# A two-layer decode step: layernorm applied after the matmul instead of before it, larger weight transfers, and a later start for part of the last weights

## Chip, cores, metric

One core of a Trainium2 chip. The metric is the device time of one execution in microseconds (us). "Span" is the part of it that the profile covers; it is some 1.7 us shorter. Ratios are the mean time of one kernel's fast runs over the mean of the fast runs of the kernel before in the same rounds on the same chip, so they are not quite the ratio of the medians that are quoted.

## The reference

Four blocks on one token x of width 1024, each with a residual: attention A, MLP B, A, B, both passes with the same weights.

```python
x = x + A(layernorm(x)); x = x + B(layernorm(x))     # pass 1
x = x + A(layernorm(x)); x = x + B(layernorm(x))     # pass 2
# A: q = xhat @ wq (32 heads of 128); softmax over the last 4096 cached keys of
#    4 kv heads; o @ wo
# B: h = xhat @ w1 + b1 (3584 wide); h * tanh(softplus(h)), called mish; @ w2
# layernorm(x) = (x - mean) / sqrt(var + 1e-5)
```

## The kernel before

PE is the matrix engine, DVE the vector engine, ACT or ScalarE the engine for functions; the sync engine (SP) issues transfers. Everything is matrix times vector: PE loads a 128x128 block of weights and multiplies it with one column; such a load with its multiplication is called a pair. wq, K, V and 20 of the 32 row blocks of wo stay in SBUF; the rest of wo, and w1 and w2, are streamed in both passes. The sync engine issues all loads in one order. Pass 1 streams through a ring of eight slots of 512 KB; in pass 2 w1 and w2 go to places that have come free: wq's (after Q), K's (after the scores), V's (after the weighted sum).

```python
# a layernorm: sums by ScalarE and DVE, a ones matmul, ten DVE steps, then Q or W1
T[f"p_lnsum{l}"] = pe.sig(p.matmul(PB_M[:, 0:2], lhsT=ones_f[:, :], rhs=st01, ...))
... # DVE: var, rsqrt by shift and two Newton steps
T[f"v_xhat{l}"] = ve.sig(v.scalar_tensor_tensor(out=xhat(l), in0=xin, scalar=MEAN,
        in1=st(8).to_broadcast([128, DC]), op0=ALU.subtract, op1=ALU.mult))
...
def emit_q(p):
    p.wait_ge(ve.sem, T[f"v_xhat{l}"])
    for j in range(DC):
        ...
        for b in range(H):
            ins = p.matmul(PB_Q[:, j * H + b:j * H + b + 1], lhsT=wq_blk(j, b),
                           rhs=XH[:, j:j + 1], start=True, stop=True)
...
# transfers
P1_K = [add_ring_piece(f"k{q}", k_piece_src(q), 16 * 128, ...) for q in range(8)]   # 512 KB
for j in range(DC):
    for half in range(2):                                  # w1 rows: 4 KiB and 3 KiB
        src, n = w1_src(j, half)
        P1_W1.append(add_ring_piece(f"w1a_{j}_{half}", src, n))
...
    elif jp < n_wq + 8:                                    # w2 of pass 2, into K's place
        dst, waits = kT_sb[:, o:o + 2048], [("T", "p_s1")]   # p_s1: scores of pass 2 done
```

## Time and profile before

| | before |
|---|---|
| median device time | 168.82 us (four runs, 168.65 to 168.88) |
| span of the profiled run | 167.1 us |
| PE / DVE / ACT busy | 53% / 19% / 8% |
| read from HBM | 57.7 MB, 345 GB/s over the span |

The span falls into two parts with different limits. Up to the last W2 piece of pass 1 (105.75 us) PE waits for data; from there on the chain that ends last has no transfer in it. The lines that show it are in the prediction below. In the lines of the chain the columns are start, duration, and what the chain went through; "issue" is an engine that waits for nothing the profile can name.

### The profile page before, as it was taken

To read this page: it belongs to the slowest core of one execution; us is meant where nothing else is said; L and a number is where in the kernel's file an instruction comes from. 1 tells how busy PE (TensorE), PEld (TensorE's weight loads), DVE (VectorE), ACT (ScalarE), POOL (GpSimd) and SP (SyncE) were. 2 spreads that over 40 slices of the span, in tenths; PEclk is the share of its full clock that TensorE was granted. 3 is DMA by queue.
4 is the path that set the end of the run, shared out by engine and by line. 5 is a ranking of instruction groups with operands and counts; after the bars stand their busy time and mean duration, and the time that the engine had idled before them with its cause. 6 is when DMAs were issued, how large, how long until landed. Compare 5 with 4: busy or idle time off the path is not lost.

```text
span 167.1 us, 5451 instructions
## 1 busy us (share of the span) xinstructions
PE 89.4 (53%) x2579; PEld 81.4 (49%) x2579; DVE 31.9 (19%) x108; ACT 13.5 (8%) x23; POOL 1.1 (1%) x11
## 2 busy tenths in 40 slices
PE   2242337956729653355433444464762963749393
PEld 1242337745718652354323333364761863749392
DVE  1400002343164000320022000330116400140402
ACT  3000000565220000000000000000001100000000
POOL 2000000000000000000000000000000000000000
PEclk9999999999655555555555555555555555555555
DMA  3999999999999999999999999999999999960000
GB/s 96 420 433 420 422 375 409 421 429 414 397 388 386 386 383 393 403 391 398 408 388 388 387 391 383 387 388 393 407 405 402 388 386 387 385 240 4 0 8 0
DMA packets 21105, 58.03 MB, mean 347 GB/s; under 512 B 1627, under 2 KB 1627, under 8 KB 19547
## 3 DMA queue, kind: packets, MB, share of 16 engines
q1 hardware_dynamic: 21082, 57.69, 89.6%
q8 instruction: 20, 0.33, 0.8%
q14 instruction: 3, 0.02, 0.0%
HBM read 57.68 MB, written 0.00 MB: 345 GB/s over the span
## 4 chain that ended last, share of the span: by engine, by line
DMA 39%; PE 30%; SPq 10%; DVE 8%; issue 7%; ACT 5%; DVEq 0%
DMA ring<-in_B_w_dram 18%; DMA ring<-in_A_k_cache_dram 13%; DMA wo_sb<-in_A_wo_dram 9%; PE psb L522 6%; SPq L662 5%; PE psb L565 4%; ACT kT_sb L614 4%; PE psb L333 4%; PE psb L599 4%; PE psb L483 3%; SPq L645 2%; PE psb L350 2%; PE psb L445 2%; PE psb L473 2%; SPq L678 2%
## 5 line engine op out<-in xcount | busy, mean ns | idle before, releaser
L333 PE MATMUL psb<-misc_b,wq_sb 128*128 128x1 bf16 x512 | 15.2, 165 | 18.6 <-DMA wq_sb<-in_A_wq_dram 14.1
L333 PEld LDWEIGHTS psb<-misc_b,wq_sb 128*128 128x128 bf16 x512 | 14.4, 104 | 19.4 <-DMA wq_sb<-in_A_wq_dram 12.2
L565 PE MATMUL psb<-act_sb,ring 128*128 128x1 bf16 x224 | 8.0, 166 | 12.1 <-DMA ring<-in_B_w_dram 9.5
L522 PE MATMUL psb<-misc_b,ring 128*128 128x1 bf16 x252 | 8.7, 166 | 10.6 <-DMA ring<-in_B_w_dram 6.3
L483 PE MATMUL psb<-misc_b,wo_sb 128*128 128x1 bf16 x320 | 9.5, 165 | 7.7 <-DMA wo_sb<-in_A_wo_dram 5.1
L522 PEld LDWEIGHTS psb<-misc_b,ring 128*128 128x128 bf16 x252 | 7.7, 105 | 11.6 <-DMA ring<-in_B_w_dram 7.1
L565 PEld LDWEIGHTS psb<-act_sb,ring 128*128 128x128 bf16 x224 | 7.0, 105 | 13.2 <-DMA ring<-in_B_w_dram 10.5
L599 PE MATMUL psb<-misc_b,ring 128*128 128x128 bf16 x128 | 10.9, 251 | 4.4 <-ACT kT_sb L614 3.6
L483 PEld LDWEIGHTS psb<-misc_b,wo_sb 128*128 128x128 bf16 x320 | 9.0, 104 | 8.0 <-DMA wo_sb<-in_A_wo_dram 5.3
L599 PEld LDWEIGHTS psb<-misc_b,ring 128*128 128x128 bf16 x128 | 9.1, 114 | 6.1 <-ACT kT_sb L614 5.1
L614 ACT ACTIVATE kT_sb<-psb 128x1024 bf16<-128x1024 bf16 x8 | 8.2, 1024 | 31.1 <-PE psb L599 31.1
L350 PE MATMUL psb<-misc_b,kT_sb 128*128 128x8 bf16 x256 | 7.3, 168 | 3.6 <-issue 3.1
L350 PEld LDWEIGHTS psb<-misc_b,kT_sb 128*128 128x128 bf16 x256 | 7.1, 104 | 3.9 <-issue 3.3
L445 PEld LDWEIGHTS psb<-et_sb,v_sb 128*128 128x128 bf16 x256 | 7.5, 105 | 1.0 <-issue 0.8
L445 PE MATMUL psb<-et_sb,v_sb 128*128 128x8 bf16 x256 | 7.6, 168 | 0.0
L609 DVE COPY kT_sb<-psb 128x1024 bf16<-128x1024 bf16 x8 | 5.5, 692 | 8.7 <-PE psb L599 8.7
L473 PE MATMUL psb<-misc_b,ring 128*128 128x1 bf16 x192 | 5.7, 165 | 2.7 <-issue 2.0
L473 PEld LDWEIGHTS psb<-misc_b,ring 128*128 128x128 bf16 x192 | 5.4, 104 | 3.0 <-issue 2.1
L359 DVE TENSOR_REDUCE misc_b<-psb 128x32 bf16<-128x256 f32 x2 | 0.8, 425 | 29.7 <-PE psb L333 29.7
L522 PE MATMUL psb<-misc_b,wq_sb 128*128 128x1 bf16 x196 | 5.5, 165 | 0.1
L522 PEld LDWEIGHTS psb<-misc_b,wq_sb 128*128 128x128 bf16 x196 | 5.4, 104 | 0.2 <-issue 0.2
L574 DVE TENSOR_REDUCE psb<-psb 128x8 f32<-128x224 f32 x2 | 0.8, 400 | 23.9 <-PE psb L565 23.9
(75 smaller groups left out, 54.8 us busy)
## 6 DMA issues: line engine op xcount, KB each, us to landing
ring<-in_B_w_dram SPq DMA_DIRECT2D x23, 512.0 KB, 10.1
wq_sb<-in_A_wq_dram SPq DMA_DIRECT2D x8, 1024.0 KB, 12.7
ring<-in_A_wo_dram SPq DMA_DIRECT2D x12, 512.0 KB, 10.6
wo_sb<-in_A_wo_dram SPq DMA_DIRECT2D x5, 1024.0 KB, 14.3
ring<-in_A_k_cache_dram SPq DMA_DIRECT2D x8, 512.0 KB, 21.6
v_sb<-in_A_v_cache_dram SPq DMA_DIRECT2D x4, 1024.0 KB, 18.7
wq_sb<-in_B_w_dram SPq DMA_DIRECT2D x8, 512.0 KB, 9.4
kT_sb<-in_B_w_dram SPq DMA_DIRECT2D x8, 512.0 KB, 10.7
```

Source lines behind the costliest of these rows:

```text
L333: ins = p.matmul(PB_Q[:, j * H + b:j * H + b + 1], lhsT=wq_blk(j, b), rhs=XH[:, j:j + 1], start=True, stop=True)
L350: ins = p.matmul(bank[:, col:col + HPG], lhsT=kT_blk(g, c), rhs=QT[:, g * HPG:(g + 1) * HPG], start=True, stop=True)
L445: ins = p.matmul(PB_O0[:, g * HPG:(g + 1) * HPG], lhsT=v_blk(g, c), rhs=et_sb[:, ecol:ecol + HPG], start=(c == 0), stop=(c == C - 1))
L473: ins = p.matmul(PB_Y[:, col:col + 1], lhsT=pc["dst"][:, o:o + 128], rhs=OT[:, j:j + 1], start=(jj == 0), stop=(jj == 1))
L483: ins = p.matmul(PB_Y[:, col:col + 1], lhsT=wo_res_blk(j, b2), rhs=OT[:, j:j + 1], start=(jj == 0), stop=(jj == 3))
L522: ins = p.matmul(PB_Q[:, j * FC + b:j * FC + b + 1], lhsT=pc["dst"][:, o:o + 128], rhs=XH[:, j:j + 1], start=True, stop=True)
L565: ins = p.matmul(PB_Y[:, j * DC + b2:j * DC + b2 + 1], lhsT=pc["dst"][:, o:o + 128], rhs=ACT_T[:, j:j + 1], start=True, stop=True)
L599: ins = p.transpose(tbk[:, k * 128:(k + 1) * 128], pc["dst"][:, o:o + 128], ident_b)
L609: T[f"v_kev{i}"] = ve.sig(v.tensor_copy(kT_sb[:, dst0:dst0 + 1024], tbk[:, 0:1024]))
L614: T[f"a_kev{i}"] = ae.sig(a.activation(kT_sb[:, dst0:dst0 + 1024], tbk[:, 0:1024], ACTF.Copy))
L645: sp.dma_start(wq_sb[:, j * 4096:(j + 1) * 4096], A_wq[j * 128:(j + 1) * 128, :]).then_inc(sem_wq[j], 16)
L662: sp.dma_start(wo_sb[:, u * 4096:(u + 1) * 4096].rearrange("p (j n) -> p j n", j=4), A_wo[u * 512:(u + 1) * 512, :].rearrange("(j p) n -> ...
```

## The change

The intent is to take the layernorm's serial DVE steps off the way between two matmuls. Since xhat = rstd * x - rstd * mean, Q and W1 can be multiplied with the raw x, and mean and rstd applied to the result; this needs the column sums of wq and w1, which a second moving column of ones delivers in pass 1 and which are kept for pass 2. Along with it come larger transfers (w1 in 896 KB, K in 1 MB, in a ring addressed by column), and one added wait. I call them (a) layernorm, (c) transfers, (d) gate; the small added DVE work is (b).

```diff
-            T[f"v_xhat{l}"] = ve.sig(v.scalar_tensor_tensor(out=xhat(l), ...))
+            T[f"v_xb{l}"] = ve.sig(v.tensor_copy(xb2(l)...[:, 0, :], xin))      # (a) raw x, before the sums
+            ve.sig(v.tensor_reduce(st01[:, 0:1], xin, AX.X, ALU.add))            # was on ScalarE
...
-            p.wait_ge(ve.sem, T[f"v_xhat{l}"])
+            nt = 2 if la == 0 else 1
+            p.wait_ge(ve.sem, T[f"v_xb{l}"])
...
+                t = ve.sig(v.tensor_reduce(QRED, PB_Q..., AX.X, ALU.add))
+            T[f"v_qt{la}"] = ve.sig(v.scalar_tensor_tensor(out=QT, in0=QRED, scalar=ln_rstd(), in1=TMPQ,
+                                                           op0=ALU.mult, op1=ALU.add))   # (b)
...
-    for j in range(DC):
-        for half in range(2):
-            src, n = w1_src(j, half)
-            P1_W1.append(add_ring_piece(f"w1a_{j}_{half}", src, n))
+    P1_W1 = [add_ring_piece(f"w1a_{j}", w1_src(j), FF) for j in range(DC)]       # (c)
+    P1_K = [add_ring_piece(f"k{g}", k_piece_src(g), C * 128, ...) for g in range(G)]
...
-            dst, waits = kT_sb[:, o:o + 2048], [("T", "p_s1")]
+            dst, waits = kT_sb[:, o:o + 2048], [("T", "p_s1"), ("T", "p_wou1_0")]   # (d)
```

`p_wou1_0` is the first of the five resident units of pass 2's output projection.

More of the change, by code (lines that the diff above doesn't have):

```diff
@@ L25 @@
 MISH_CLAMP = 20.0
-NSLOT = 8
 WO_RES = 20
-SLOT = 2048
+RING_COLS = 16384
+NSEM_RING = 12
+STAGE_COLS = 256
 class _Eng:
@@ L53, in _build @@
     v_sb = E(nc.sbuf_tensor("v_sb", [128, G * C * DH], BF16))
-    ring = E(nc.sbuf_tensor("ring", [128, NSLOT * SLOT], BF16))
+    ring = E(nc.sbuf_tensor("ring", [128, RING_COLS], BF16))
     ones_f = E(nc.sbuf_tensor("ones_f", [128, 128], F32))
-    misc_b = E(nc.sbuf_tensor("misc_b", [128, 512], BF16))
-    misc_f = E(nc.sbuf_tensor("misc_f", [128, 320], F32))
+    misc_b = E(nc.sbuf_tensor("misc_b", [128, 576], BF16))
+    misc_f = E(nc.sbuf_tensor("misc_f", [128, 448], F32))
     act_sb = E(nc.sbuf_tensor("act_sb", [128, 2 * FC], BF16))
@@ L62, in _build @@
     ident_b = misc_b[:, 128:256]
-    MB_XH = 256
+    MB_XB2 = 512
     MB_QT = 288
@@ L79, in _build @@
     MF_DD = 286
+    MF_CSQ = 320
+    MF_CS1 = 352
+    MF_TMPQ = 380
+    MF_BB = 412
     def cfc(i):
@@ L86, in xT, with xb2 @@
         return misc_f[:, MF_XS + i * DC:MF_XS + (i + 1) * DC]
-    def xhat(l):
-        return misc_b[:, MB_XH + l * DC:MB_XH + (l + 1) * DC]
+    def xb2(l):
+        return misc_b[:, MB_XB2 + l * 2 * DC:MB_XB2 + (l + 1) * 2 * DC]
     PB = [E(nc.psum_tensor(f"psb{i}", [128, 512], F32)) for i in range(8)]
@@ L102, in _build @@
     XS_RED2 = 496
+    XS_QRED = 96
     pe = _Eng(E(nc.semaphore("sem_pe")))
@@ L112, in _build @@
     sem_wo = [E(nc.semaphore(f"dma_wo{i}")) for i in range(WO_RES // 4)]
-    sem_slot = [E(nc.semaphore(f"dma_slot{i}")) for i in range(NSLOT)]
+    sem_ring = [E(nc.semaphore(f"dma_ring{i}")) for i in range(NSEM_RING)]
     sem_dbg = E(nc.semaphore("dma_dbg")) if dbg is not None else None
@@ L117, in _build @@
     pieces = []
-    ring_count = [0]
+    ring_pieces = []
+    ring_state = dict(off=0)
     def add_ring_piece(name, src, ncols, shape3=None):
-        ridx = ring_count[0]
-        ring_count[0] += 1
-        s, r = ridx % NSLOT, ridx // NSLOT
-        pc = dict(name=name, ring=True, ridx=ridx, slot=s, round=r, sem=sem_slot[s], val=16 * (r + 1),
-                  dst=ring[:, s * SLOT:s * SLOT + ncols], src=src, shape3=shape3, issue_waits=[])
+        idx = len(ring_pieces)
+        if ring_state["off"] + ncols > RING_COLS:
+            ring_state["off"] = 0
+        start = ring_state["off"]
+        end = start + ncols
+        assert end <= RING_COLS
+        ring_state["off"] = end
+        overl = [q for q in ring_pieces if q["start"] < end and start < q["end"]]
+        pc = dict(name=name, ring=True, ridx=idx, start=start, end=end, sem=sem_ring[idx % NSEM_RING],
+                  val=16 * (idx // NSEM_RING + 1), dst=ring[:, start:end], src=src, shape3=shape3, issue_waits=[],
+                  overlap=overl[-1] if overl else None,
+                  sem_prev=ring_pieces[idx - NSEM_RING] if idx >= NSEM_RING else None,
+                  stage_overlap=(end > RING_COLS - STAGE_COLS))
         pieces.append(pc)
+        ring_pieces.append(pc)
         return pc
@@ L142, in _build, with k_piece_src @@
     SRC = {}
-    def k_piece_src(q):
-        g, half = divmod(q, 2)
-        ap = A_k_cache[0, g, SK - WIN:SK, :].rearrange("(p c) d -> p c d", c=C)[:, half * 16:(half + 1) * 16, :]
-        return ap
+    def k_piece_src(g):
+        return A_k_cache[0, g, SK - WIN:SK, :].rearrange("(p c) d -> p c d", c=C)
     def v_src(g):
@@ L153, in wo_pair_src, with w1_src @@
         return A_wo[jp * 256:(jp + 1) * 256, :].rearrange("(j p) n -> p j n", p=128)
-    def w1_src(j, half):
-        c0 = 0 if half == 0 else 2048
-        n = 2048 if half == 0 else FF - 2048
-        return B_w1[j * 128:(j + 1) * 128, c0:c0 + n], n
+    def w1_src(j):
+        return B_w1[j * 128:(j + 1) * 128, :]
     def w2_pair_src(jp):
         return B_w2[jp * 256:(jp + 1) * 256, :].rearrange("(j p) n -> p j n", p=128)
-    P1_K = [add_ring_piece(f"k{q}", k_piece_src(q), 16 * 128, shape3=(16, 128)) for q in range(8)]
+    P1_K = [add_ring_piece(f"k{g}", k_piece_src(g), C * 128, shape3=(C, 128)) for g in range(G)]
     NWO_STR = (H - WO_RES) // 2
     P1_WO = [add_ring_piece(f"wo1_{jp}", wo_pair_src(WO_RES // 2 + jp), 2048, shape3=(2, 1024)) for jp in range(NWO_STR)]
-    P1_W1 = []
-    for j in range(DC):
-        for half in range(2):
-            src, n = w1_src(j, half)
-            P1_W1.append(add_ring_piece(f"w1a_{j}_{half}", src, n))
+    P1_W1 = [add_ring_piece(f"w1a_{j}", w1_src(j), FF) for j in range(DC)]
     P1_W2 = [add_ring_piece(f"w2a_{jp}", w2_pair_src(jp), 2048, shape3=(2, 1024)) for jp in range(FC // 2)]
     P2_WO = [add_ring_piece(f"wo2_{jp}", wo_pair_src(WO_RES // 2 + jp), 2048, shape3=(2, 1024)) for jp in range(NWO_STR)]
-    P2_W1 = []
     wq_off = [0]
@@ L177, in wq_alloc @@
         o = wq_off[0]
-        wq_off[0] += 2048
-        unit_last = (o + 2048 - 1) // 4096
+        wq_off[0] += ncols
+        unit_last = (o + ncols - 1) // 4096
+        assert wq_off[0] <= DC * 4096
         return wq_sb[:, o:o + ncols], unit_last
-    for j in range(DC):
-        for half in range(2):
-            src, n = w1_src(j, half)
-            idx = 2 * j + half
-            if idx < NSLOT - NWO_STR:
-                P2_W1.append(add_ring_piece(f"w1b_{j}_{half}", src, n))
-            else:
-                dst, u = wq_alloc(n)
-                P2_W1.append(add_direct_piece(f"w1b_{j}_{half}", dst, src, issue_waits=[("T", f"p_qfree{u}")]))
+    P2_W1 = [add_ring_piece("w1b_0", w1_src(0), FF)]
+    p2_prior = P1_K + P1_WO + P1_W1 + P1_W2
+    if P2_W1[0]["overlap"] is not None and P2_W1[0]["overlap"] not in p2_prior:
+        bad = P2_W1.pop()
+        pieces.remove(bad)
+        ring_pieces.remove(bad)
+        dst, u = wq_alloc(FF)
+        P2_W1.append(add_direct_piece("w1b_0", dst, w1_src(0), issue_waits=[("T", f"p_qfree{u}")]))
+    for j in range(1, DC):
+        dst, u = wq_alloc(FF)
+        P2_W1.append(add_direct_piece(f"w1b_{j}", dst, w1_src(j), issue_waits=[("T", f"p_qfree{u}")]))
     P2_W2 = []
+    n_wq = (DC * 4096 - wq_off[0]) // 2048
     for jp in range(FC // 2):
-        n_wq = (DC * 4096 - wq_off[0]) // 2048
         if jp < n_wq:
@@ L202, in _build @@
         P2_W2.append(add_direct_piece(f"w2b_{jp}", dst, w2_pair_src(jp), shape3=(2, 1024), issue_waits=waits))
-    assert wq_off[0] <= DC * 4096
+    for pc in P2_WO + [q for q in P2_W1 if q["ring"]]:
+        assert pc["overlap"] is None or pc["overlap"] in p2_prior, pc["name"]
+        assert pc["sem_prev"] is None or pc["sem_prev"] in p2_prior, pc["name"]
     def wq_blk(j, b):
@@ L219, in v_blk @@
         return v_sb[:, o:o + 128]
-    STAGE = ring[:, (NSLOT - 1) * SLOT:NSLOT * SLOT]
+    STAGE = ring[:, RING_COLS - STAGE_COLS:RING_COLS]
     et_sb = E(nc.sbuf_tensor("et_sb", [128, 1024], BF16))
@@ L237, in _ @@
         g.memset(cfc(C2), 2.0)
+        g.memset(misc_b[:, MB_XB2:MB_XB2 + 8 * DC], 1.0)
         T["g_consts"] = ge.sig(g.memset(cfc(CCL), MISH_CLAMP))
@@ L256, in _, with lnstats @@
         T["v_b1T"] = ve.sig(v.tensor_copy(PB_X[:, XS_B1T:XS_B1T + FC], PB_Q[:, DC:DC + FC]))
-    def layernorm(l, xin):
+    def lnstats(l, xin):
         def st(a, n=1):
@@ L266, in _ @@
             v.wait_ge(ve.sem, ve.n)
+            T[f"v_xb{l}"] = ve.sig(v.tensor_copy(xb2(l).rearrange("p (j t) -> p t j", t=2)[:, 0, :], xin))
+            ve.sig(v.tensor_reduce(st01[:, 0:1], xin, AX.X, ALU.add))
             T[f"v_lnstat{l}"] = ve.sig(v.tensor_tensor_reduce(
                 out=sq, in0=xin, in1=xin, scale=1.0, scalar=0.0, op0=ALU.mult, op1=ALU.add, accum_out=st01[:, 1:2]))
-        @block.scalar
-        def _(a):
-            a.wait_ge(ve.sem, T[f"v_x{l}"])
-            T[f"a_lnstat{l}"] = ae.sig(a.activation(misc_b[:, 488:488 + DC], xin, ACTF.Copy,
-                                                    accum_out=st01[:, 0:1]))
         @block.tensor
@@ L278, in _ @@
             p.wait_ge(ve.sem, T[f"v_lnstat{l}"])
-            p.wait_ge(ae.sem, T[f"a_lnstat{l}"])
             T[f"p_lnsum{l}"] = pe.sig(p.matmul(PB_M[:, 0:2], lhsT=ones_f[:, :], rhs=st01, start=True, stop=True))
@@ L303, in _, with ln_rstd, ln_nmr @@
                 y = ynew
-            T[f"v_xhat{l}"] = ve.sig(v.scalar_tensor_tensor(out=xhat(l), in0=xin, scalar=MEAN,
-                                                            in1=st(8).to_broadcast([128, DC]),
-                                                            op0=ALU.subtract, op1=ALU.mult))
+            T[f"v_ln{l}"] = ve.sig(v.tensor_scalar(st(9), MEAN, st(8), -1.0, ALU.mult, ALU.mult))
+    def ln_rstd():
+        return misc_f[:, MF_LN + 8:MF_LN + 9]
+    def ln_nmr():
+        return misc_f[:, MF_LN + 9:MF_LN + 10]
     def s_view(bank):
@@ L321, in layer_A @@
         MBC = misc_f[:, MF_MBC:MF_MBC + H]
-        XH = xhat(l)
-        layernorm(l, xin)
+        XB2 = xb2(l)
+        CSQ = misc_f[:, MF_CSQ:MF_CSQ + H]
+        TMPQ = misc_f[:, MF_TMPQ:MF_TMPQ + H]
+        lnstats(l, xin)
         def emit_q(p):
-            p.wait_ge(ve.sem, T[f"v_xhat{l}"])
+            nt = 2 if la == 0 else 1
+            p.wait_ge(ve.sem, T[f"v_xb{l}"])
             for j in range(DC):
@@ L332, in emit_q @@
                 for b in range(H):
-                    ins = p.matmul(PB_Q[:, j * H + b:j * H + b + 1], lhsT=wq_blk(j, b), rhs=XH[:, j:j + 1],
+                    col = (j * H + b) * nt
+                    ins = p.matmul(PB_Q[:, col:col + nt], lhsT=wq_blk(j, b), rhs=XB2[:, 2 * j:2 * j + nt],
                                    start=True, stop=True)
@@ L356, in emit_qt @@
         def emit_qt(v):
-            v.wait_ge(pe.sem, T[f"p_q{la}"])
-            with nc.allow_low_precision("fp32 accumulate, bf16 store of Q^T"):
-                T[f"v_qt{la}"] = ve.sig(v.tensor_reduce(QT, PB_Q[:, 0:DC * H].rearrange("p (j b) -> p b j", j=DC),
-                                                        AX.X, ALU.add))
+            QRED = PB_X[:, XS_QRED:XS_QRED + H]
+            if la == 0:
+                qv = PB_Q[:, 0:2 * DC * H].rearrange("p (j b t) -> p t b j", j=DC, b=H, t=2)
+                v.wait_ge(pe.sem, T[f"p_q{la}"])
+                t = ve.sig(v.tensor_reduce(CSQ, qv[:, 1, :, :], AX.X, ALU.add))
+                v.wait_ge(ve.sem, t)
+                v.wait_ge(ve.sem, T[f"v_ln{l}"])
+                ve.sig(v.tensor_scalar(TMPQ, CSQ, ln_nmr(), None, ALU.mult))
+                t = ve.sig(v.tensor_reduce(QRED, qv[:, 0, :, :], AX.X, ALU.add))
+            else:
+                v.wait_ge(ve.sem, T[f"v_ln{l}"])
+                ve.sig(v.tensor_scalar(TMPQ, CSQ, ln_nmr(), None, ALU.mult))
+                v.wait_ge(pe.sem, T[f"p_q{la}"])
+                t = ve.sig(v.tensor_reduce(QRED, PB_Q[:, 0:DC * H].rearrange("p (j b) -> p b j", j=DC), AX.X, ALU.add))
+            v.wait_ge(ve.sem, t)
+            T[f"v_qt{la}"] = ve.sig(v.scalar_tensor_tensor(out=QT, in0=QRED, scalar=ln_rstd(), in1=TMPQ,
+                                                           op0=ALU.mult, op1=ALU.add))
         if after_q is None:
-            vqt_pred = ve.n + 1
+            vqt_pred = ve.n + 3
             @block.tensor
@@ L484, in _ @@
                                        start=(jj == 0), stop=(jj == 3))
-            T[f"p_y{la}"] = pe.sig(ins)
+                T[f"p_wou{la}_{u}"] = pe.sig(ins)
+            T[f"p_y{la}"] = pe.n
         @block.vector
@@ L497, in layer_B @@
     def layer_B(l, lb, xin, xout, w1_pieces, w2_pieces):
-        XH = xhat(l)
+        XB2 = xb2(l)
         ACT_T = act_sb[:, lb * FC:(lb + 1) * FC]
@@ L504, in layer_B @@
         DD = misc_f[:, MF_DD:MF_DD + FC]
+        CS1 = misc_f[:, MF_CS1:MF_CS1 + FC]
+        BB = misc_f[:, MF_BB:MF_BB + FC]
+        compute_cs = (lb == 0)
         def hcol(k):
             return PB_X[:, hs0 + k * FC:hs0 + (k + 1) * FC]
-        layernorm(l, xin)
+        lnstats(l, xin)
+        nt = 2 if compute_cs else 1
         @block.tensor
         def _(p):
-            p.wait_ge(ve.sem, T[f"v_xhat{l}"])
-            for k, pc in enumerate(w1_pieces):
-                j, half = divmod(k, 2)
-                bs = range(0, 16) if half == 0 else range(16, FC)
-                b0 = bs[0]
+            p.wait_ge(ve.sem, T[f"v_xb{l}"])
+            for j, pc in enumerate(w1_pieces):
                 pwait(p, pc)
                 ins = None
-                for b in bs:
-                    o = (b - b0) * 128
-                    ins = p.matmul(PB_Q[:, j * FC + b:j * FC + b + 1], lhsT=pc["dst"][:, o:o + 128],
-                                   rhs=XH[:, j:j + 1], start=True, stop=True)
+                for b in range(FC):
+                    col = (j * FC + b) * nt
+                    ins = p.matmul(PB_Q[:, col:col + nt], lhsT=pc["dst"][:, b * 128:(b + 1) * 128],
+                                   rhs=XB2[:, 2 * j:2 * j + nt], start=True, stop=True)
                 consumed(pc, pe.sig(ins))
+                T[f"p_h{lb}_{j}"] = pe.n
             T[f"p_h{lb}"] = pe.n
@@ L528, in _ @@
         def _(v):
+            if not compute_cs:
+                v.wait_ge(ve.sem, T[f"v_ln{l}"])
+                ve.sig(v.scalar_tensor_tensor(out=BB, in0=CS1, scalar=ln_nmr(), in1=PB_X[:, XS_B1T:XS_B1T + FC],
+                                              op0=ALU.mult, op1=ALU.add))
             v.wait_ge(pe.sem, T[f"p_h{lb}"])
-            t = ve.sig(v.tensor_reduce(RED, PB_Q[:, 0:DC * FC].rearrange("p (j b) -> p b j", j=DC), AX.X, ALU.add))
+            if compute_cs:
+                hv2 = PB_Q[:, 0:2 * DC * FC].rearrange("p (j b t) -> p t b j", j=DC, b=FC, t=2)
+                t = ve.sig(v.tensor_reduce(RED, hv2[:, 0, :, :], AX.X, ALU.add))
+                t = ve.sig(v.tensor_reduce(CS1, hv2[:, 1, :, :], AX.X, ALU.add))
+                v.wait_ge(ve.sem, t)
+                v.wait_ge(ve.sem, T[f"v_ln{l}"])
+                t = ve.sig(v.scalar_tensor_tensor(out=BB, in0=CS1, scalar=ln_nmr(), in1=PB_X[:, XS_B1T:XS_B1T + FC],
+                                                  op0=ALU.mult, op1=ALU.add))
+            else:
+                t = ve.sig(v.tensor_reduce(RED, PB_Q[:, 0:DC * FC].rearrange("p (j b) -> p b j", j=DC), AX.X, ALU.add))
             v.wait_ge(ve.sem, t)
-            t = ve.sig(v.tensor_tensor(HH, RED, PB_X[:, XS_B1T:XS_B1T + FC], ALU.add))
+            t = ve.sig(v.scalar_tensor_tensor(out=HH, in0=RED, scalar=ln_rstd(), in1=BB, op0=ALU.mult, op1=ALU.add))
             v.wait_ge(ve.sem, t)
@@ L580, in k_transposes, with _ @@
         for i in range(nb):
-            q, bi = divmod(i, 2)
-            pc = P1_K[q]
-            g, half = divmod(q, 2)
-            cs = [16 * half + 8 * bi + k for k in range(8)]
+            g, bi = divmod(i, 4)
+            pc = P1_K[g]
+            cs = [8 * bi + k for k in range(8)]
             tbk = TBK[i % 2]
             @block.tensor
-            def _(p, i=i, pc=pc, g=g, cs=cs, tbk=tbk, bi=bi, half=half):
+            def _(p, i=i, pc=pc, g=g, cs=cs, tbk=tbk, bi=bi):
                 if bi == 0:
@@ L597, in _ @@
                 for k, c in enumerate(cs):
-                    o = (c - 16 * half) * 128
-                    ins = p.transpose(tbk[:, k * 128:(k + 1) * 128], pc["dst"][:, o:o + 128], ident_b)
+                    ins = p.transpose(tbk[:, k * 128:(k + 1) * 128], pc["dst"][:, c * 128:(c + 1) * 128], ident_b)
                 T[f"p_ktr{i}"] = pe.sig(ins)
-                if bi == 1:
+                if bi == 3:
                     consumed(pc, T[f"p_ktr{i}"])
@@ L645, in _ @@
             sp.dma_start(wq_sb[:, j * 4096:(j + 1) * 4096], A_wq[j * 128:(j + 1) * 128, :]).then_inc(sem_wq[j], 16)
-        slot_prev = {NSLOT - 1: T["p_xb1"]}
         order = []
@@ L669, in _ @@
             if pc["ring"]:
-                prev = slot_prev.get(pc["slot"])
-                if prev is not None:
-                    sp.wait_ge(pe.sem, prev)
-                slot_prev[pc["slot"]] = pc["consumed"]
+                waits = []
+                if pc["overlap"] is not None:
+                    waits.append(pc["overlap"]["consumed"])
+                if pc["sem_prev"] is not None:
+                    waits.append(pc["sem_prev"]["consumed"])
+                if pc["stage_overlap"]:
+                    waits.append(T["p_xb1"])
+                if waits:
+                    sp.wait_ge(pe.sem, max(waits))
             dst = pc["dst"]
```

## The prediction

> **What bounds the kernel now.** I read the 40 slices first, then the critical chain in order of time, then the engine timeline of the second pass, then small windows of the DMA view.
>
> The slices (one is 4.2 us) show where the DMA stops being the bound:
>
> ```profile
> span 167.1 us, 5451 instructions
> PE   2242337956729653355433444464762963749393
> DMA  3999999999999999999999999999999999960000
> ```
>
> The DMA is full until slice 35 (about 147 us), and the tensor engine is half idle there. The chain tells where one bound hands over to the other:
>
> ```profile
> 95.61 10.14 DMA ring<-in_B_w_dram
> 105.75 0.04 issue
> 105.79 0.60 PE psb L565 x16
> ...
> 110.23 3.84 PE psb L333 x138
> 114.07 2.30 issue
> 116.37 3.30 PE psb L333 x118
> ...
> 120.61 1.96 issue
> ...
> 134.52 0.98 issue
> 135.50 2.56 PE psb L473 x90
> 138.06 1.01 PE psb L483 x38
> 139.07 2.63 issue
> 141.69 3.43 PE psb L483 x122
> ```
>
> The last step that waits for data is the last W2 piece of pass 1, landed at 105.75. After it no step of the chain waits for a transfer: 61 us of compute on weights already there. So the first 106 us count bytes, the last 61 count PE and DVE steps, and a change is worth something only if it speeds bytes before 106 or shortens the chain after. The "issue" entries, 7.9 us in the four long ones, are the third thing to see: PE stands still waiting for nothing named, every 128 load/multiply pairs (118 + 10, then 90 + 38). The last thing is the layernorm bubble, here of layer 3 in the timeline of PE:
>
> ```profile
> 146.08 0.56 PE L280 MATMUL psb<-misc_f,ones_f 128*128 128x2 f32 x2 [0.97 <-ACT misc_b L273]
> 148.81 0.91 PE L522 MATMUL psb<-misc_b,ring 128*128 128x1 bf16 x28 [2.17 <-DVE misc_b L304]
> ```
>
> PE ends the sums at 146.64 and waits 2.17 us for ten small DVE steps (L287 to L304); before layer 2's Q (L333) it is 2.18 us.
>
> [...] (128 pairs are 256 instructions; 20 packets make 0.33 MB) [...] 139 to 142 us has one such packet
>
> ```profile
> q8 instruction: 1, 0.02, 2.3%
> ```
>
> inside the stall of 139.07. From block to block that fetch took 135.50 to 141.69 = 6.2 us, though PE eats a block in 3.6. Once the DMA had thinned out (148.9 to 152.6) it took about 3.7 and the stall was 0.14. [...] two moving columns should cost what one costs. The trace agrees: eight columns 168 ns (L350), one column 165 (L333), small DVE ops 0.15 to 0.3 us. [...] Over 2 KiB runs (86 to 106 us) the trace has 387 GB/s, over W1's 4 and 3 KiB (66 to 84) 400, over wq's 8 KiB (4 to 20) 424.
>
> **The change part by part.**
>
> (a) *Layernorm taken off the way.* PE multiplies raw x; mean and rstd are applied after the reduce. In PE's order the sums' matmul still comes first, so PE still waits for it. In front of it ScalarE's accumulate (it ended the wait) gives way to a copy and a reduce on DVE; independent DVE ops start about 0.1 us apart here (145.63, 145.73), so the sums start within 0.1 us of where they did. Then Q or W1 starts at once: gain 2.17, less nothing, say 2.15 each. In pass 2 both lie on the chain: 2 x 2.15 = 4.3 us. In pass 1 layer 0 waits for wq and layer 1 for W1's transfers: 0.
>
> (b) *Added DVE work.* In pass 2 the mean term is computed under the matmuls; what stays is one op after Q's reduce, 0.25 us (a 128x28 op of this kind, L544, is 0.26), and 0.05 in W1's (a three-operand op in place of an add). The 0.25 falls before the scores' fetch stall, whose end is paced by the fetch, so it vanishes there. Pass 1's two-column matmuls and doubled reduces (0.42 each) lie under transfers: 0.
>
> (c) *Larger transfers.* W1 goes as 7 KiB rows, K as 8 KiB. W1 has 7.34 MB a pass: at 400 GB/s 18.35 us, at an estimated 418 17.55. So 0.8 us before 105.75. K ran at about the rate of V already; I count nothing. In pass 2 it only helps (d).
>
> (d) *A moved gate.* The eight W2 pieces into K's buffer waited for pass 2's scores (125.88); now also for the first resident unit of its output projection. Ahead of the gate lie Wo 3.15 + W1 7.34 + three W2 pieces 1.57 = 12.06 MB. Total traffic from 106 to the end was 16.81 MB of 17.83, so 1.02 had moved by then; the other 11.04 last at old rates to 134.0 (106 to 134 moved 11.09). Less 0.8 from (c) twice: 132.4. PE's chain up to the output projection comes 2.9 us early (0.8 + 2.15), so its fetch stall ends near 132.6 and the gate opens after 118 more pairs of 28 ns, at 135.9. With some 1.8 us from issue to steady traffic (wq was issued at 1.54 and its bytes flow from about 3.3) the DMA has a hole from about 133 to 137.8. The block asked for at 132.6 now meets an emptying queue; at 3.7 us it is there when needed (136.2), so the 2.63 us stall goes. But the last 11 pieces (5.77 MB, 14.9 us at 388) then run until about 153, over W1 of pass 2, where the block boundary (7 pairs into W1, by the order of instructions) meets a full queue: PE needs it 3.6 us later and gets it after 6.2, a new stall of 2.5 (0.14 before). W2 reaches V's buffer near 157.5, after its data.
>
> Sum: -0.8 (c) -4.3 (a) +0.05 (b) -2.6 +2.4 (d) = -5.3. From 168.82: 163.5. I say 163.7, leaning to the side where larger pieces leave fewer bytes in flight in the ring.
>
> **The rivals.**
> 1. *The fetch stalls take it back.* If the queue isn't empty when the block is asked for at 132.6 (transfers of engines that lag: the DMA of the kernel before thinned out over 3.5 us, 146.8 to 150.3), the old stall stays and the new one is added: -0.8 -4.3 +2.4 = -2.7, 166.1. For: the estimate of the hole is good to 1 to 2 us only. Against: traffic thins before it ends, and two shifts widen the hole.
> 2. *The new stall doesn't come*, because the fetch at W1 gets through better: -7.7, 161.1. Against: all full-queue fetches that PE outran took 5.3 to 6.2 us.
> 3. *Pass 1 starves.* 7 KiB pieces are freed 0.9 MB at a time. With about 2.75 MB in flight at an issue, of which some 1 MB has moved before its semaphore shows, about 1.5 us of margin remain. If it fails, (c) turns from -0.8 to +0.5: 164.9. The DMA row would drop under 9 around 75 to 90 us.
> 4. *It is hidden anyway.* The DMA is full most of the time, so nothing is gained. Against: 61 us of the chain hold no transfer.
> 5. *W2's data becomes the bound* because of the late gate: the last piece would have to land after 158. My margin is 3 us.
>
> **Range and chances.** (a) is the sure part: two bubbles seen in the trace, 4.3 us. (c) is 0 to 1.2. (d) lies between -2.6 and +2.5, centred near 0. So 161.4 to 166.3 for 8 in 10. The 2% line is 165.44, which needs (a) to be kept and (d) not to go fully wrong: 0.83 faster, 0.16 within, 0.01 slower.
>
> **What would show it right or wrong.** (a): under 0.2 us idle between the sums' matmul and the first Q and W1 matmul of pass 2. (c): the last W2 wait of pass 1 ends near 105. (b): pass-2 scores start about 2.6 us earlier. (d): a dip in the DMA row near 133 to 138, transfers to about 153, no issue gap in the resident output projection, one of about 2.5 us some 135 pairs into W1. Wrong if PE waits for a DMA after 106 us, if the bubble comes back as a wait for the copy of x, or if pass 1 ends later than 106.

## The result

| | before | after |
|---|---|---|
| median device time | 168.80 us (15 runs) | 162.60 us (11 runs, one of them slow) |
| ratio | | 0.9631, 95% interval 0.9609 to 0.9652 |
| span of the profiled run | 167.1 us | 161.7 us |
| last wait for a W2 piece of pass 1 ends | 105.75 us | 104.48 us |

The change is faster by 3.7%, 1.1 us below the 163.7 us that were predicted. The profiled run of the changed kernel is one of its longer ones (163.51 us), so the traces explain 5.4 us of the 6.2 by which the medians differ. Its page:

```profile
span 161.7 us, 5442 instructions
PE   2242254966575975454441444475762969576392
DMA  3999999999999999999999999999999953899700
```

The hole in the DMA row (slices 32 and 33, about 130 to 138 us) is the gate; the transfers now thin out from 152 us and end by 154. PE's pace is the same in both kernels (128 pairs take 3.6 us, at a granted clock of 0.50 from 106 us on), so the clock is no rival. The same chain as in the prediction, changed kernel:

```profile
94.31 10.17 DMA ring<-in_B_w_dram
104.48 0.05 issue
...
106.79 3.79 PE psb L349 x142
110.58 1.93 issue
112.50 3.21 PE psb L349 x114
...
117.05 1.65 issue
...
130.64 0.98 issue
131.63 2.46 PE psb L502 x87
134.08 4.33 PE psb L512 x160
...
140.12 0.72 issue
140.85 3.57 PE psb L554 x128
144.42 2.62 issue
```

And the timeline of PE where the layernorm of layer 2 stood, changed kernel:

```profile
106.21 0.58 PE L288 MATMUL psb<-misc_f,ones_f 128*128 128x2 f32 x2 [1.10 <-DVE misc_f L282]
106.65 3.92 PE L349 MATMUL psb<-misc_b,wq_sb 128*128 128x1 bf16 x142
```

The bubble is gone: Q follows the sums at once. The gap of 2.63 us in the output projection is gone too (L512 runs its 160 pairs in one piece), and two gaps have come up in W1 (L554), 0.72 and 2.62.

Read side by side, the two traces tell a simple story. The end of pass 1 came 1.27 us earlier. Two bubbles of 2.2 us went. The long gaps add up to 8.0 us in both (2.30 + 1.96 + 0.98 + 2.63 + 0.14 before, 1.93 + 1.65 + 0.98 + 0.72 + 2.62 + 0.11 after). So the layernorm would have made 4.3 of the 5.4 us, and the gate nothing. That is also how the prediction had divided it. The experiments say otherwise.

### The profile page after: what moved, and what is told of

Its sections match the earlier page's. It is cut to its first block, busy times and chain, and to the rows that moved or that the text cites.

```text
span 161.7 us, 5442 instructions
## 1 busy us (share of the span) xinstructions
PE 88.5 (55%) x2579; PEld 81.0 (50%) x2579; DVE 34.6 (21%) x124; ACT 12.3 (8%) x15; POOL 1.2 (1%) x12
## 4 chain that ended last, share of the span: by engine, by line
DMA 40%; PE 36%; issue 8%; DVE 6%; ACT 5%; SPq 3%; DVEq 0%
DMA ring<-in_B_w_dram 26%; DMA ring<-in_A_k_cache_dram 14%; PE psb L554 5%; PE psb L611 5%; PE psb L366 5%; ACT kT_sb L658 4%; PE psb L643 4%; PE psb L349 4%; PE psb L474 4%; PE psb L502 4%; PE psb L512 3%; SPq L689 2%; DVE psb L449 1%; DVE misc_b L424 1%; PE psb L462 1%
## 5 line engine op out<-in xcount | busy, mean ns | idle before, releaser
L349 PE MATMUL psb<-misc_b,wq_sb 128*128 128x2 bf16 (+1 forms) x512 | 15.2, 165 | 15.9 <-DMA wq_sb<-in_A_wq_dram 14.0
L554 PE MATMUL psb<-misc_b,ring 128*128 128x2 bf16 (+1 forms) x252 | 8.3, 166 | 9.5 <-DMA ring<-in_B_w_dram 8.7
L554 PEld LDWEIGHTS psb<-misc_b,ring 128*128 128x128 bf16 x252 | 7.8, 106 | 10.1 <-DMA ring<-in_B_w_dram 9.3
L512 PE MATMUL psb<-misc_b,wo_sb 128*128 128x1 bf16 x320 | 9.5, 165 | 3.3 <-DMA wo_sb<-in_A_wo_dram 2.4
L512 PEld LDWEIGHTS psb<-misc_b,wo_sb 128*128 128x128 bf16 x320 | 9.0, 104 | 3.6 <-DMA wo_sb<-in_A_wo_dram 2.7
L502 PE MATMUL psb<-misc_b,ring 128*128 128x1 bf16 x192 | 5.7, 165 | 2.7 <-issue 2.0
L554 PE MATMUL psb<-misc_b,wq_sb 128*128 128x1 bf16 x196 | 5.5, 165 | 2.6 <-issue 2.6
L554 PEld LDWEIGHTS psb<-misc_b,wq_sb 128*128 128x128 bf16 x196 | 5.4, 104 | 2.7 <-issue 2.7
## 6 DMA issues: line engine op xcount, KB each, us to landing
ring<-in_A_wo_dram SPq DMA_DIRECT2D x12, 512.0 KB, 10.7
```

The source lines that it names most:

```text
L349: ins = p.matmul(PB_Q[:, col:col + nt], lhsT=wq_blk(j, b), rhs=XB2[:, 2 * j:2 * j + nt], start=True, stop=True)
L502: ins = p.matmul(PB_Y[:, col:col + 1], lhsT=pc["dst"][:, o:o + 128], rhs=OT[:, j:j + 1], start=(jj == 0), stop=(jj == 1))
L512: ins = p.matmul(PB_Y[:, col:col + 1], lhsT=wo_res_blk(j, b2), rhs=OT[:, j:j + 1], start=(jj == 0), stop=(jj == 3))
L554: ins = p.matmul(PB_Q[:, col:col + nt], lhsT=pc["dst"][:, b * 128:(b + 1) * 128], rhs=XB2[:, 2 * j:2 * j + nt], start=True, stop=True)
```

## The experiments

My theory after the result was that of the prediction: (a) is worth 4.3 us, (c) what the end of pass 1 moved, (d) nearly nothing. The rival: the instruction fetch sets the pace of pass 2, so that a removed bubble is mostly filled by a fetch gap, and the gain comes from the hole in the traffic. The first four runs take the parts one by one. "Before" had a median of 168.72 us in these rounds.

**Run 1, (c) alone.** The changed kernel with the old layernorm put back and the gate left out.

```diff
-            p.wait_ge(ve.sem, T[f"v_xb{l}"])
+            p.wait_ge(ve.sem, T[f"v_xhat{l}"])          # and the old layernorm with it
-            ... [("T", "p_s1"), ("T", "p_wou1_0")]
+            ... [("T", "p_s1")]
```

> Part (c) alone: W1 as 896 KB pieces and K as 1 MB pieces in the byte-addressed ring, the old layernorm and no moved gate. If the parts add up as I reckon, it is worth what the end of pass 1 moved in the changed kernel, 1.27 us: 167.5 us, with the last W2 wait of pass 1 ending near 104.5 and the layernorm bubbles of 2.2 us still there. The rival that the larger transfers made the gain would give 163 to 164 us.

Measured: 167.40 us, ratio 0.9916 (0.9896 to 0.9936); the last W2 wait of pass 1 ends at 104.56. As expected: what the end of pass 1 moves, 1.2 us, comes through.

**Run 2, (a) alone.** The kernel before with the new layernorm, its transfers as they were (the diff is the layernorm hunks of the change).

> Part (a) alone on the old pieces and the old order of transfers. Two bubbles of 2.15 us go, 4.3 us. But the DMA then still runs (to about 150 us) when W1 of pass 2 begins near 144.6, so the block fetch there should cost a stall of about 1 us that the kernel before did not have: 165.6 us. If fetch stalls do not depend on the traffic, 164.5. If the layernorm bubble was hidden, 168.8.

Measured: 167.98 us, ratio 0.995 (0.9931 to 0.997), so 0.7 us of gain where I expected 3.2. The trace tells where the rest went. Up to the output projection the chain is 2.7 us ahead of the kernel before. Then W1 of pass 2 starts at 143.9 us, while the transfers run until about 150, and it meets gaps of 1.54 and 2.62 us where the kernel before, whose W1 started at 148.8 as the traffic thinned out, had one of 0.14. That is 4.0 us of gaps for a bubble of 2.2.

**Run 3, (a) and (c), no gate.**

```diff
-            dst, waits = kT_sb[:, o:o + 2048], [("T", "p_s1"), ("T", "p_wou1_0")]
+            dst, waits = kT_sb[:, o:o + 2048], [("T", "p_s1")]
```

> The changed kernel without the added wait of the eight W2 pieces on the output projection (parts a and c). By my sum the gate is nearly neutral (-2.6 and +2.4): between 162.6 and 164.5, with the 2.6 us stall back in the resident output projection, no hole in the DMA row, transfers done near 148 and the stall in W1 down to 0.5 to 2 us; best guess 164.0. The rival that the hole in the traffic is a main source of the gain would give 165 us or more.

Measured: 166.86 us, ratio 0.9887 (0.9867 to 0.9907). This is outside what I had allowed for a neutral gate: with it the ratio is 0.9631, so this one wait is worth 2.6% or 4.3 us; it is the rival that I had put at 165 us or more. The chain without it:

```profile
134.08 1.09 PE psb L512 x41
135.17 2.65 issue
137.81 3.33 PE psb L512 x119
...
142.86 1.27 issue
144.13 3.57 PE psb L554 x128
147.70 2.62 issue
```

The gap in the output projection is back (2.65), and W1 has its two gaps as well (1.27 and 2.62). I had charged W1's gap to the gate, as its price. It comes without the gate too. These gaps are what the gate is worth in the traces: 2.65 and 0.55 us, 3.2 in all, for profiled runs that differ by 3.1 (166.64 and 163.51).

**Run 4, (c) and (d), the old layernorm.** As run 1, the gate left in.

> The changed kernel with the old layernorm (parts c and d). If (a) is worth 4.3 us in the presence of the rest: 162.6 + 4.3 = 166.9 us; by the sum of the parts 168.8 - 1.3 - 2.6 + 2.4 = 167.3. If the bubble is partly taken up by fetch stalls (the fetch runs during the bubble, so that removing it only moves the wait), (a) is worth less here: 165 to 166.

Measured: 165.44 us (164.55 to 166.72), ratio 0.9781 (0.975 to 0.9812). With the gate in place the layernorm is worth 2.8 us, not 4.3. Put together:

| parts | median us | against before |
|---|---|---|
| (c) | 167.40 | -1.3 |
| (a) | 167.98 | -0.7 |
| (a) (c) | 166.86 | -1.9 |
| (c) (d) | 165.44 | -3.3 |
| (a) (c) (d), the change | 162.60 | -6.2 |

The gate gives 2.0 us without the new layernorm and 4.3 with it; the new layernorm gives 0.5 us without the gate (166.86 against 167.40) and 2.8 with it. The parts don't add up; each makes room for the other. The gate alone, and the gate with (a) on the old transfers, were not run.

**Run 5, one bubble put back.** The changed kernel; W1 of pass 2 waits for the end of the layernorm chain of layer 3 again, though it doesn't use its result.

```diff
-            p.wait_ge(ve.sem, T[f"v_xb{l}"])
+            p.wait_ge(ve.sem, T[f"v_xb{l}" if lb == 0 else f"v_ln{l}"])
```

> The changed kernel, but W1 of pass 2 again waits for the end of the layernorm of layer 3 (the wait alone is put back; same arithmetic). If the hidden layernorm of layer 3 is worth its 2.15 us, 164.8. If the block fetch sets the pace there (in the changed kernel W1 stalls 0.72 + 2.62 us; with the bubble, in the run of transfers and gate, 0.42), the bubble only replaces the stalls: 162 to 163 us, the same as 162.6, with issue gaps under 1 us in W1.

Measured: 163.33 us, ratio 0.966 (0.9624 to 0.9696; the change has 0.9609 to 0.9652). The intervals overlap: by the medians the 2.2 us bubble costs 0.7 us, by the far ends of the intervals anything from nothing to 1.5, and the two profiled runs even lie the other way (162.22 with the bubble, 163.51 without). W1 in its chain:

```profile
141.88 3.76 PE psb L554 x135
145.64 0.36 issue
146.00 2.54 PE psb L554 x89
```

With the bubble (139.74 to 141.88, 2.14 us), W1's gaps shrink from 0.72 + 2.62 to 0.36, as they would if the block is fetched while PE waits for the layernorm. So of (a) it is layer 2's bubble that pays: run 4 has both bubbles, this run has one, and they differ by 2.1 us (165.44 and 163.33; different chips, on which the kernel before had 168.72 and 168.87). This is a comparison of two runs that differ in the layernorm's arithmetic too; layer 2's bubble alone was not put back.

**Run 6, are the gaps block fetches?** 64 dummy pairs in pass 1, where PE is idle.

```diff
+            if lb == 0:
+                for _k in range(NDUMMY):      # 64, before W2 of layer 1
+                    p.matmul(PB_Y[:, 300:301], lhsT=ident_b, rhs=ident_b[:, 0:1], start=True, stop=True)
```

> The changed kernel with 64 dummy load/multiply pairs in pass 1, where PE waits for the mish of layer 1 anyway (1.8 us of 3.2 idle), so that every later block boundary falls 64 pairs earlier in the algorithm. If the issue gaps are block fetches, they move: Q's gap from pair 142 to 206, the scores' from 14 to 78, W1's from 7 and 135 to 71 and 199. Time 162 to 165 us. If the gaps belong to a place in the algorithm (a bank, a buffer, a wait), they stay at their pairs and the time stays at 162.6.

Measured: 165.23 us, ratio 0.9777 (0.9749 to 0.9804). Timeline of PE; the last bracket of a row is the idle time before it:

```profile
106.58 5.63 PE L350 MATMUL psb<-misc_b,wq_sb 128*128 128x1 bf16 x206
114.33 1.49 PE L350 MATMUL psb<-misc_b,wq_sb 128*128 128x1 bf16 x50 [2.12 <-issue]
116.64 2.24 PE L367 MATMUL psb<-misc_b,kT_sb 128*128 128x8 bf16 x78 [0.81 <-DVE misc_b L389]
120.25 1.50 PE L367 MATMUL psb<-misc_b,kT_sb 128*128 128x8 bf16 x50 [1.37 <-issue]
```

Q's gap moved from pair 142 to 206 and the scores' from 14 to 78, by 64 each; W1's moved to pairs 71 and 199 (28 + 43, then 128 more). The gaps hang on the count of instructions, not on a place in the algorithm. That they are fetches of the next block of instructions can be seen in the DMA view, where instructions have a queue of their own. The view of 147 to 148 us of this run, inside W1's second gap (147.04 to 149.67), has one packet of it (columns: packets, MB, share of the 16 engines):

```profile
q8 instruction: 1, 0.02, 7.0%
```

By the packed traces of the two kernels and the twelve runs, each of the 75 "issue" gaps of PE of over 0.1 us after 105 us ends 1.2 to 1.6 us after such a packet of 16,384 bytes has landed; the only others, one of 0.24 us in each of eight traces, lie beside a matmul whose record is missing.

The time is 2.6 us above the change, and just outside the 162 to 165 us that I gave. The traces show 0.8 us of it (gaps of 8.8 us in all against 8.0; profiled runs of 164.41 and 163.51 us); the rest I can't place.

**Runs 7 and 8, fewer bytes in flight.** No gate; the sync engine issues a piece of pass 2's w1 and w2 only when the one three (run 8: two) before it has landed.

```diff
+            if not pc["ring"] or pc["name"] == "w1b_0":
+                paced.append(pc)
+                if len(paced) > DEPTH:          # 3 or 2
+                    q = paced[-1 - DEPTH]
+                    sp.wait_ge(q["sem"], q["val"])
```

> The changed kernel without the gate; instead the last transfers (W1 and W2 of pass 2) are issued only when the piece three before has landed, so at most three (2.75 or 1.5 MB) are in flight in place of some 4 MB. If the fetch's wait grows with the bytes queued, the gaps (11.7 us in all without the gate) shrink to about half: 161 to 163 us. If it is only a matter of the engines being busy, they stay: 166 to 167.5 us.

> As the run with three in flight, with two (1.8 or 1.0 MB). If the fetch's wait grows with the bytes queued: gaps of under 1 us each and 157 to 161 us, or, if the data then comes too late, waits for DMA in W2. If not, gaps as before and 166 to 168 us.

Measured: three in flight 162.92 us, ratio 0.9655 (0.9631 to 0.968), so 2.3% better than run 3 without any gate; its gaps after the scores add up to 3.9 us, those of run 3 to 7.5. Two in flight 172.32 us, ratio 1.014 (1.0053 to 1.0227; one of its four runs was slow). In run 8 the gaps after Q's nearly vanish (1.67 in Q, then 0.28, 0.18 and 0.49 us) and W2 starts at 147.2, 5 us earlier than in the changed kernel; but the rate falls to 242 GB/s from 128 to 146 us (run 3: 378 from 130 to 146), and W2 waits for data, eight times and 12.7 us in all. The chain goes through the transfers (the 4.74 us are a transfer's, not PE's wait, which is 2.36 us here):

```profile
148.78 4.74 DMA kT_sb<-in_B_w_dram
```

So the fetch's time does depend on the data traffic in flight (6.19 to 6.31 us for a block without a limit, 4.55 and 4.83 in runs 7 and 8, see the table below), and giving up traffic has a price. The "some 4 MB" of the expectation are an estimate: in the kernel before a 512 KB piece of pass 2's w2 into K's place took 10.7 us from issue to landing, at 387 GB/s from 130 to 146 us, which makes 4.1 MB.

**Runs 9 and 10, the same bytes in finer pieces.** As run 7, each piece in two halves with a semaphore each; at most 4 w1 and 6 w2 halves (run 10: 3 and 5) in flight.

```diff
+                for h in range(2):
+                    if len(sent) >= depth:      # D1 = 4 for w1, D2 = 6 for w2; run 10: 3 and 5
+                        sp.wait_ge(sent[-depth], 16)
+                    ...
+                    sp.dma_start(d, sr).then_inc(sem, 16)
```

> No gate; the transfers of pass 2 go as halves (W1 512 and 384 KB, W2 256 KB) and at most 4 W1 halves (1.8 MB) or 6 W2 halves (1.6 MB) are in flight. If what matters to a block fetch is the bytes queued ahead of it (4.6 to 4.8 us per block at 1.5 to 1.8 MB, 6.2 at 4 MB), the gaps in W1 and the output projection fall to about 1 us each, while finer pieces keep the rate near 385 GB/s so that the data is done by about 149: 160.5 to 162 us. If the fetch minds only whether the engines are full, the gaps stay at 2.6 and the time near 166.

> As the run before with 3 W1 halves (1.4 MB) and 5 W2 halves (1.3 MB) in flight. By the same theory gaps of about 0.6 us, a rate near 330 GB/s, data done near 154: 159 to 161.5 us; if the rate falls under 300, PE waits for W2's data as in the run with two in flight, and it is 164 or more.

Measured: run 9 162.17 us, ratio 0.9604 (0.9563 to 0.9644), the lowest of all, though not clearly below the change. Its chain in the output projection and W1:

```profile
133.84 1.50 issue
135.35 3.33 PE psb L513 x119
...
140.38 0.45 issue
140.83 3.57 PE psb L557 x128
144.41 0.43 issue
```

The gaps are 1.50 in the output projection and 0.45 and 0.43 in W1, in place of 2.65, 1.27 and 2.62 in run 3. The rate did not hold near 385 GB/s as expected; it fell to between 290 and 390, and the transfers end near 154 us, while W2 runs. Run 10: 165.48 us, ratio 0.9805 (0.9774 to 0.9837); W1's gaps are down to 0.17 and 0.15, and W2 waits for data eight times, 3.4 us in all. That was the miss I had named; of these settings run 9 has the best balance.

One fetch, from the end of one gap to the end of the next, can be read from these chains where PE outran it (PE needs 3.57 us for a block); the start of its packet is in the packed traces:

| run | w1 or w2 allowed in flight | one block fetch, us | of it, until its packet starts, us |
|---|---|---|---|
| before, change, run 3 | not limited | 6.19 to 6.31 | 3.6 to 4.0 |
| runs 4 and 6 | in the gate's hole | 4.00 and 3.73 | 1.1 and 1.1 |
| run 7 | 1.5 MB of w2 | 4.55 | 2.2 |
| run 8 | 1.8 MB of w1 | 4.83 | 2.4 |
| run 9 | 1.6 MB of w2 in 256 KB halves | 5.48, 4.01 | 3.1, 1.6 |
| run 10 | 1.3 to 1.4 MB in halves | 4.83, 5.21, 3.73 | 2.6, 2.8, 1.3 |

The packet itself takes 0.9 to 1.2 us in 71 of the 75 fetches. What changes is how long it waits before it starts: 1.1 us where the DMA stands still (run 6: 16 GB/s from 134 to 135 us), almost 4 in full traffic (before: 387 GB/s from 130 to 146 us). As the packet starts after PE has entered a block, and PE needs what it brings 128 pairs (3.57 us) later, this fits a fetch of one block ahead. The limit alone does not give the number (run 9 has 5.48 and 4.01 at the same one). Nor do these runs tell bytes queued ahead from engines that are less busy, because the rate fell along with the limit (378 GB/s in run 3, 338 in run 9, 300 and 293 in runs 7 and 10, from 130 to 146 us).

**Runs 11 and 12, what of (c) is K's.** Run 11 sends K in the eight half pieces of the kernel before, the rest as in the change.

```diff
-    P1_K = [add_ring_piece(f"k{g}", k_piece_src(g), C * 128, ...) for g in range(G)]
+    P1_K = [add_ring_piece(f"k{q}", k_piece_src(q), 16 * 128, ...) for q in range(2 * G)]
```

> The changed kernel with K again in eight 512 KB pieces of 4 KiB rows. It tells what of the 1.27 us by which pass 1 ended earlier is K's: if K's larger rows give nothing, as I counted, the last W2 wait of pass 1 ends at 104.5 and the time is 162.6; if they give the part that I did not count (0.5), it ends at 105.0 and the time is 163.1.

Measured: 164.01 us, ratio 0.971 (0.9684 to 0.9736); the last W2 wait ends at 105.6. So 1.1 of the 1.27 us are K's, which I had counted as nothing, by this measure. It is clear of the noise: the ten profiles of these experiments that have K in 1 MB pieces (the failed run 12 apart) end that wait between 104.4 and 104.7 us. The DMA view of 22 to 26 us, first of the changed kernel, then of run 11:

```profile
DMA packets 239, 1.70 MB, mean 424 GB/s; under 512 B 32, under 2 KB 32, under 8 KB 32
```

```profile
DMA packets 329, 1.43 MB, mean 356 GB/s; under 512 B 37, under 2 KB 37, under 8 KB 273
```

With halves the rate dips as the traffic changes from wq to K (356 in place of 424 GB/s; the kernel before has 365), and later halves of K run at full rate again (414 and 426 GB/s from 30 to 34 us). By bytes moved up to 106 us W1 has its share as well: 41.2 MB before, 41.4 in run 11, 41.7 in the change, so about 0.24 MB (0.6 us) from W1's larger rows and 0.30 MB (0.8 us) from K. In run 11 most of W1's share does not show in the landing of the last piece; I leave that open.

Run 12 was to tell row length from transfer size: K in 512 KB transfers, but of 64 partitions with rows of 8 KiB.

```diff
+                sp.dma_start(dst[0:64], pc["src"][0:64]).then_inc(pc["sem"], 16)
+                sp.dma_start(dst[64:128], pc["src"][64:128]).then_inc(pc["semx"], 16)
```

> The changed kernel with each K piece sent as two transfers of 64 partitions: 512 KB each, as before, but rows of 8 KiB, as in the changed kernel. It tells row length from transfer size. If the row length makes the difference of the run with K in halves (350 to 380 GB/s at 22 to 26 us in place of 418 to 430, and 1.1 us at the end of pass 1), this one behaves like the changed kernel: last W2 wait near 104.5, 162.6 us. If the size of the transfer makes it: the dip at 22 to 26 us again, last W2 wait near 105.6, 164.0 us.

Measured: 174.36 us, ratio 1.0293 (1.0242 to 1.0344). The experiment failed, because it changed a second thing: a transfer covers 64 partitions in place of 128. DMA view of 26 to 42 us:

```profile
DMA packets 530, 3.51 MB, mean 219 GB/s; under 512 B 103, under 2 KB 103, under 8 KB 103
```

The changed kernel has 421 GB/s in this window. So with K over 64 partitions at a time the rate was about half, 219 against 421, while the view shows the DMA engines fully busy in both (100.4% and 100.9% for the data queue). Why was not shown. Whether K's gain is row length or transfer size stays open.

## Why the prediction was right, and where it was not

**(a) the bubbles.** The first half of the mechanism is as predicted: the sums start 0.43 us after x is ready (105.78 to 106.21; 0.45 before), and Q and W1 follow at once. (The two DVE starts that the prediction reads as independent ops, 145.63 and 145.73, are one operation and the read of its accumulator; the conclusion held all the same.) The size was right only as a difference of two timelines. "The sure part ... 4.3 us" failed: the same edit gives 0.7 us alone (run 2), 2.8 us in the change (run 4), and layer 3's bubble alone 0.7 by the medians (run 5). The step that failed is "In pass 2 both lie on the chain: 2 x 2.15". Layer 3's bubble lay on the chain, but beside a block fetch that would have ended the wait next: in the kernel before, the block that PE enters 3 pairs into W1 landed at 146.65 us, and PE goes on 1.2 to 1.6 us after a landing, so by this estimate it would have stood until about 148 of the 148.81 us without the bubble too. Layer 2's bubble has no such block beside it; the one that PE enters 10 pairs into Q had landed at 101.3 us.

**(b) the added DVE work.** The size was right: 0.26 us after Q's reduce (L388), and the scores' gap fell from 1.96 to 1.65, so it is absorbed there. Two moving columns did cost what one costs (166 and 165 ns in the changed kernel). The scores of pass 2 start 3.7 us earlier and not 2.6, because pass 1 ended earlier than reckoned and Q took 0.5 us less, most of it in a shorter gap (2.30 to 1.93).

**(c) the transfers.** Predicted -0.8, with nothing from K; measured -1.27 at the end of pass 1, and -1.3 in time (run 1). The step that was mis-sized is "K ran at about the rate of V already; I count nothing": by landing 1.1 us of it are K's. The rate of W1 was near (415 GB/s from 68 to 82 us in the changed kernel, 399 before). The 418 of the prediction was an estimate, between the 400 and the 424 GB/s that it read for rows of 4 and 3 KiB and of 8 KiB. By rows the traces have 387 GB/s with 2 KiB, 399 with 4 and 3 KiB, 415 with 7 KiB and 424 with 8 KiB, each from another stage of the kernel. Rival 3, starvation, did not show (its 1.5 us of margin were an estimate, from the 2.75 MB in flight and the 1 MB moved that it names); the DMA row holds its nines.

**(d) the gate.** The events came as worked out: a hole in the traffic (predicted 133 to 137.8; measured under 40 GB/s from 133 to 136), no gap in the output projection, transfers until about 153, a gap of 2.62 us (predicted 2.5) at pair 135 of W1. I had missed the 0.72 at pair 7. But the price of "+2.4" was put on the wrong part. Run 3 shows that W1's gaps come without the gate too (1.27 + 2.62), because the shorter chain of (a) brings W1 into the time when the transfers still run. So the gate is worth 4.3 us beside (a) and 2.0 without it, not nothing, and (a) pays the 2.4. The sum was near because I had worked out one joint timeline; the division among parts was wrong, and reading the two traces side by side would have confirmed it. That the sum came out so near is in part luck. Against the prediction the traces have 0.5 us more from (c) and 0.7 more from shorter gaps in Q and the scores, and 0.9 less from unforeseen gaps in W1 and W2 and 0.3 less from (b), which nearly cancel.

**The rivals.** 1 (the old gap stays and the new one is added) is just what run 3 shows without the gate: 166.86, where it said 166.1. 2 is ruled out: W1's gap came. 4 is half true, run 2: most of what the layernorm frees is taken again, not by transfers that PE waits for but by an instruction fetch that is slow while transfers run (gaps of 1.54 and 2.62 us where the kernel before had 0.14). What 5 feared, W2 waiting for its data, came in runs 8 and 10, from the limit on transfers and not from the gate.

## What to carry to other kernels

When a stage has an idle "issue" gap every fixed number of instructions, look for the longer of the work and the fetch between two boundaries: here 3.57 us and, in full traffic, about 6.2. A bubble inside it was nearly free (layer 3's of 2.2 us cost 0.7 by the medians, run 5), and without it W1 had 4.0 us more of gaps (run 2); so shorten the fetch first. Where the data has time to spare, holding back transfers over a short stage, or keeping fewer bytes in flight, can be worth more than the arithmetic that is saved (against run 3, the gate gave 4.3 us and run 7's limit 3.9; the layernorm gave 2.8 against run 4). And a sum of parts that comes out right is no proof of the parts: run them one by one.
